# Attention and a rational-activation MLP on one core: bias moved from sigmoids to logarithms, four units masked, new planner costs, contiguous inputs

## The chip, the cores and the metric

The kernel runs on one core of a Trainium2 chip. The metric is the device time of one execution, in microseconds, as the median of a few runs.

## The reference

Two stages follow each other. In the first, 32 learned vectors attend over each batch's 12480 tokens (4 batches, 128 channels), and then the tokens attend over the 32 results. In the second, every token goes through an MLP with 2048 hidden units whose activation is a rational function of h.

```python
def mab(q, kv):
    s = scale * (q @ kv.transpose(0, 2, 1))
    s = s - s.max(-1, keepdims=True)
    a = np.exp(s)
    a /= a.sum(-1, keepdims=True) + 1e-09
    return a @ kv
h = mab(I, x)
return mab(x, h)
...
h = x @ w_in
P = a[0] + a[1] * h + a[2] * h2 + a[3] * h3
Q = 1.0 + np.abs(b[0]) * np.abs(h) + np.abs(b[1]) * h2
g = P / (Q + 1e-6)
return g @ w_out
```

## The kernel before

**The work.** Tokens are cut into tiles of 480 (26 a batch, 104 in all), and the hidden layer into 8 pairs of 128 units. One tile with one pair is a unit, `Unit(b, n, q)`, 832 in all. Since the attention's output is a mix of 32 vectors, `piece` multiplies those vectors with `w_in` once per batch into the stationary matrix `st`, and `first` gets a unit's h by two matmuls of `st` with the 128-row tile `at`, which holds the attention weights of the tile's tokens in parts.

**A unit's way.** `first` (PE) writes h into one of three PSUM banks. Then |h| is taken, in one of two ways. In a unit whose q is not in `MASKED`, the stationary matrix already holds a shift by `k2`, and ACT takes the absolute value with the bias `back` that takes it out again ("abs", `u<-h,all`). DVE then makes the numerator's product D from u and h. In a unit whose q is in `MASKED`, there is no shift; DVE clears the sign bit ("mask", `u<-h` on DVE), or ACT takes a plain absolute value ("taken", `u<-h` on ACT), and POOL prepares u + k1 ("pre", `l<-u,all`) before D (`l<-h,all,l`). For a q that is also in `EXTRA`, PE can instead compute the shifted h a second time from the extra weights `sx` ("again"), and D takes the other form, without "pre". D frees the bank. Next, 1/Q comes as a sigmoid of a logarithm: ACT takes Ln over two units at once ("ln", `u<-u 128x1920`) and then a Sigmoid: two units at once ("sig2"), one ("sig", `u<-u,all 128x960`), or one into a PSUM bank ("sigp", `i<-u,all`). After a sigmoid into PSUM, DVE adds k3 and multiplies ("Ev", `l<-l,all,i`); after the others POOL does, in two instructions ("add", `l<-l,all`, and "Eg", `l<-l,u`). `second` (PE) multiplies the result with `w_out` in two fp32 matmuls of two passes each, adding up over the tile's 8 units in the bank po, and `fetch` copies it out (DVE) and stores it.

Ln and Sigmoid are in different activation tables, so ACT works in batches of up to six pairs: a table load, six Ln, a table load, twelve sigmoids.

**Order.** All engines work in order. The class `Flow` plans the order when the program is built: it keeps a clock per engine, and at each step picks among the events that could come next (`options`), by ready time and by the tables `COST` (how long each event is taken to be), `RANK`, `LOAD`, `GEN` and `WAIT`. `do` emits the instructions. The attention of coming tiles (`tokens`, `quotients`, `spread`) and the next batch's first stage (`induce`) run as generators between the units. Loads go out on SP's queue. `InOrder.do`, line 157, records every instruction of the fast branch, so nearly all rows of the profile name that line.

**The start.** `before()` loads all of batch 0 by columns (`wide_columns`) and by rows (`x_rows`, 512 B runs in `x_t`) and the weights as float64 words, converts these (`words`), computes the first attention, and derives the activation's constants (`Params.derive`): with c2 = ch - 1, the sigmoid has the bias `lnc` = ln(c2) + 2 ln(LAM), one number held in a column of the tile `all`. The logarithm's bias is the constant LAM.

Of the kernel before, what the change touches and what calls it, by code (L numbers as in the profile page):

```python
# [17 lines left out]
P = 128  # L18
# [3 lines left out]
HB = 4  # L22
# [22 lines left out]
class Params:  # L45
# [46 lines left out]
    def derive(self):  # L92

        a0, a1, a2, a3 = self.a
        mult, add, sub, mx = ALU.mult, ALU.add, ALU.subtract, ALU.max
        b0, b1 = self.ts(self.b0, 1e-3, mx), self.ts(self.b1, 1e-3, mx)
        mag3 = self.abs(a3)  # L100
# [12 lines left out]
        r = self.mul(r, self.kappa)
        q1 = self.mul(a1, r)
        r = self.mul(r, self.kappa)
        q0 = self.mul(a0, r)
        self.k1 = self.ts(self.sub(ch, q1), 0.5, mult)
        k12 = self.mul(self.k1, self.k2)
        self.k3 = self.sub(self.ts(self.sub(self.mul(self.k2, ch), q0), 0.5, mult), k12)
        self.back = self.ts(self.k2, -1.0, mult)  # L120
        top = self.mul(self.mul(self.mul(a3, alpha), self.mul(alpha, alpha)), self.recip(gamma))
        self.rho = self.ts(self.mul(top, self.recip(c2)), -2.0, mult)
        self.lin_scale = self.ts(self.mul(c2, self.kappa), -0.5, mult)
        self.lin_shift = self.ts(self.mul(c2, self.k2), -0.5, mult)
        self.lnc = self.new()
        self.nc.scalar.activation(self.lnc, c2, AF.Ln, bias=0.0, scale=1.0)
        self.lnc = self.ts(self.lnc, 2.0 * math.log(LAM), add)
# [52 lines left out]
class Flow:  # L180


    LAT = 0.15
    COST = {"first": 0.52, "second": 1.53, "linear": 0.3, "again": 0.52, "fetch": 0.6, "D": 1.13, "mask": 1.08, "Ev": 1.13, "abs": 0.95, "ln": 1.71, "sig": 1.79, "half": 0.99, "load": 1.4, "pre": 1.1, "add": 1.13, "Eg": 2.22}
    RANK = {"again": 2.9, "first": -30.3, "second": 86.6, "fetch": -52.7, "D": 10.9, "mask": -30, "Ev": -53.2, "abs": 3, "ln": 64.3, "wide": 100, "one": 2, "sig": -64.7, "pre": -41.2, "add": 113.3, "Eg": 74.2, "load": 34, "take": 71.3}
    LOAD = {"v": -2.15, "g": -0.03}
    GEN = {"pe": 3.3, "v": 59.3, "a": 7.9, "g": 26.8, "x": -49.5}
    WAIT = {"pe": 0, "v": 0, "a": 0, "g": 0.2}
    BATCH = 6
# [6 lines left out]
    BANKS = 3  # L196
    FULL = 12.7
    MASKED = (0, 2, 3, 5, 6)
    EXTRA = (2, 5)

# [84 lines left out]
    def options(self):  # L285
# [9 lines left out]
        if self.i1 < len(us) and bank is not None and self.free(self.slots) is not None and (self.i1 % 2 or self.free(self.rooms) is not None):  # L295
            u = us[self.i1]
            at = self.k.ready_at(u)
            if at is not None:
                yield "pe", max(at, bank), R["first"], C["first"], ("first", u)
        if self.i2 < len(us):  # L300
# [16 lines left out]
        for u in self.masks[:1]:  # L317
            yield "a", max(u.t["first"] + LAT, u.room_at), R["take"], C["abs"], ("taken", u)
        for u in self.abss[:1]:
# [28 lines left out]
    def do(self, what, u, start, end):  # L348
# [75 lines left out]
        elif what == "ln":  # L424
            w = us[2 * u]
            A.activation(w.pair, w.pair, AF.Ln, bias=LAM, scale=LAM)
            self.nl += 1
            self.since = end
        elif what == "sig2":
            A.activation(u.pair, u.pair, AF.Sigmoid, bias=p.lnc, scale=-2.0)  # L430
            for w in us[u.n:u.n + 2]:
# [4 lines left out]
        elif what == "sig":  # L436
            A.activation(u.u, u.u, AF.Sigmoid, bias=p.lnc, scale=-2.0)
            u.t["e"] = end + LAT
# [3 lines left out]
        elif what == "sigp":  # L442
            u.bank, _ = self.take(self.banks)
            u.inv = k.hp(u, "i")
            A.activation(u.inv, u.u, AF.Sigmoid, bias=p.lnc, scale=-2.0)
            u.t["e"] = end + LAT
# [40 lines left out]
class Kernel:  # L487

    def __init__(self, ctx, tc, x_t, x_c, ind_c, w_in_d, w_out_d, moe_a, moe_b, out):
        self.tc, self.nc = tc, Engines(tc)  # L490
        self.x_t, self.x_c, self.ind_c, self.w_in_d, self.w_out_d = x_t, x_c, ind_c, w_in_d, w_out_d
        self.moe_a, self.moe_b, self.out = moe_a, moe_b, out
        self.B, _, self.NCH, _ = x_t.shape
        self.NB = self.NCH // HB
        self.NG = -(-self.NB // 4)
        self.F = w_in_d.shape[1]
        self.NF = self.F // P
# [50 lines left out]
    def weights(self):  # L548

        parts = []  # L550
        for f0 in range(0, self.F, BT):
            c = slice(f0, min(f0 + BT, self.F))
            parts.append((self.w_in_d[:, c], self.w_in[:, c], c.stop - c.start))
        for f0 in range(0, self.NF, 3):
            c = slice(f0, min(f0 + 3, self.NF))
            dst = self.w_out[:, c].rearrange("p f d -> p (f d)")
            parts.append((self.w_out_d[:, c].rearrange("p f d -> p (f d)"), dst, C * (c.stop - c.start)))
        for n, (src, dst, width) in enumerate(parts):
            tag, bufs = (self.place("l"), 1) if width > 2 * P else ("oT", 1)
            raw = self.mp.tile([P, width], mybir.dt.int64, tag=tag, name=f"raw{n}", bufs=bufs)  # L560
            self.nc.sync.dma_start(out=raw, in_=src)
            yield raw, dst, width
# [307 lines left out]
    def quotients(self, b, n0, nb, a):  # L870
# [269 lines left out]
```

## Time and profile before

| | before |
|---|---|
| median of 3 runs | 2376.53 us (2374.88 to 2377.35) |
| profiled execution | 2380.21 us, span 2378.4 us |
| PE busy | 2181.4 us, 92% of the span |
| ACT busy | 2149.8 us, 90% |
| DVE busy | 2128.0 us, 89% |
| POOL busy | 2008.2 us, 84% |
| mean granted TensorE clock | 0.958 of full speed |

The span runs from the first to the last instruction; the execution's own time is 1.8 us longer. The profile's views used below are the page with busy time per engine, the groups of instructions by form (busy time, mean length of one), the windows view (busy time of each engine in a stretch), the waits (who waited for whom), the chain of work that ended last, and the DMA view. PE is TensorE's matmuls, DVE VectorE, ACT ScalarE, POOL GpSimd. Matmuls overlap, so PE's busy time is not the time it needs at its peak.

### The profile page before, as it was taken

How to read it: one execution, taken by the hardware profiler on the slowest of the kernel's cores; microseconds unless marked ns; L12 is line 12 of the kernel's file. 1: busy time of each engine (PE TensorE's matmuls, PEld its weight loads, DVE VectorE, ACT ScalarE, POOL GpSimd, SP SyncE). 2: the span in 40 equal slices, each digit the busy share in tenths (PEclk: the TensorE clock that was granted, in tenths of full speed). 3: DMA queues.
4: the chain of work that ended last, by engine and by line, in shares of the span. 5: the costliest groups of instructions: out<-in, count | busy, mean ns of one | idle time of the engine just before them, and what ended most of it. 6: DMA issues, size and time to landing. Idle time of an engine off the chain costs nothing.

```text
span 2378.4 us, 24506 instructions
## 1 busy us (share of the span) xinstructions
PE 2181.4 (92%) x7930; PEld 1209.7 (51%) x7930; DVE 2128.0 (89%) x2289; ACT 2149.8 (90%) x1782; POOL 2008.2 (84%) x1406
## 2 busy tenths in 40 slices
PE   6688999999998999899999999999999998989898
PEld 3454545554554555454555555455455554545444
DVE  5668999999899899998999999999999889979996
ACT  1479999999999999998999999999999989989997
POOL 1268998979999899888999888897999999889995
PEclk7669999999999999999999999999999999999999
DMA  9112212211102222220111122222110111011000
GB/s 282 42 46 75 75 51 75 83 42 40 35 25 77 67 73 75 75 58 25 42 42 59 50 75 75 70 61 61 42 42 21 38 42 42 25 34 34 26 25 19
DMA packets 78640, 133.72 MB, mean 56 GB/s; under 512 B 13544, under 2 KB 63976, under 8 KB 78504
## 3 DMA queue, kind: packets, MB, share of 16 engines
q1 hardware_dynamic: 78504, 132.06, 18.8%
q8 instruction: 66, 1.08, 0.2%
q14 instruction: 70, 0.57, 0.1%
HBM read 80.89 MB, written 25.56 MB: 45 GB/s over the span
## 4 chain that ended last, share of the span: by engine, by line
PE 44%; DVE 23%; ACT 14%; POOL 9%; issue 6%; DMA 1%; SPq 1%; ACTq 0%; DVEq 0%; POOLq 0%
PE po L157 29%; DVE l L157 14%; ACT u L157 9%; PE h L157 9%; POOL l L157 9%; DVE u L157 5%; ACT i L157 3%; PE pd L157 2%; PE ph L157 2%; ACT L157 1%; DVE asm L157 1%; DMA at<-hl 1%; SPq L157 1%; DVE oT L157 1%; PE pl L157 1%
## 5 line engine op out<-in xcount | busy, mean ns | idle before, releaser
L157 PE MATMUL po<-l,w_out 128*128 128x480 f32 x3328 | 1496.8, 583 | 36.8 <-POOL l L157 17.7
L157 POOL TENSOR_TENSOR l<-l,u 128x960 f32<-128x960 f32 x451 | 1011.8, 2244 | 41.9 <-ACT u L157 17.2
L157 PEld LDWEIGHTS po<-l,w_out 128*128 128x128 f32 x3328 | 623.1, 193 | 573.7 <-issue 465.3
L157 PE MATMUL h<-at,st 128*128 128x480 f32 x1664 | 655.7, 488 | 100.0 <-DVE l L157 87.4
L157 ACT ACTIVATE u<-u 128x1920 f32<-128x1920 f32 x416 | 731.0, 1799 | 9.3 <-DVE l L157 8.2
L157 POOL TENSOR_SCALAR l<-u,all 128x960 f32<-128x960 f32 x435 | 464.3, 1069 | 218.2 <-DVE u L157 160.6
L157 DVE TENSOR_SCALAR u<-h 128x960 int32<-128x960 int32 x447 | 508.4, 1150 | 70.4 <-PE h L157 65.6
L157 DVE SCALAR_TENSOR_TENSOR l<-h,all,l 128x960 f32<-128x960 f32 x435 | 520.7, 1208 | 25.9 <-POOL l L157 24.1
L157 DVE SCALAR_TENSOR_TENSOR l<-u,all,h 128x960 f32<-128x960 f32 x397 | 476.0, 1205 | 37.9 <-ACT u L157 28.7
L157 PEld LDWEIGHTS h<-at,st 128*128 128x128 f32 x1664 | 300.5, 194 | 393.2 <-issue 203.7
L157 DVE SCALAR_TENSOR_TENSOR l<-l,all,i 128x960 f32<-128x960 f32 x381 | 450.5, 1207 | 41.9 <-ACT i L157 40.9
L157 POOL TENSOR_SCALAR l<-l,all 128x960 f32<-128x960 f32 x451 | 482.6, 1070 | 1.0
L157 ACT ACTIVATE u<-u,all 128x1920 f32<-128x1920 f32 (+1 forms) x299 | 441.1, 1492 | 0.2
L157 ACT ACTIVATE i<-u,all 128x960 f32<-128x960 f32 x381 | 396.9, 1056 | 31.3 <-DVE l L157 28.3
L157 ACT ACTIVATE u<-h,all 128x960 f32<-128x960 f32 x312 | 327.8, 1051 | 40.0 <-PE h L157 38.8
L157 ACT ACT_TABLE_LOAD x148 | 189.9, 1283 | 3.4 <-PEq L1133 0.7
L157 PEld LDWEIGHTS pd<-HT,xT 128*120 128x120 f32 x832 | 109.1, 196 | 20.7 <-issue 11.7
L157 PE MATMUL pd<-HT,xT 128*120 128x32 f32 x832 | 103.1, 271 | 3.8 <-issue 2.4
L157 ACT ACTIVATE u<-h 128x960 f32<-128x960 f32 x73 | 70.1, 963 | 29.5 <-PE h L157 26.2
L157 DVE COPY oT<-po 128x480 f32<-128x480 f32 x104 | 67.6, 650 | 17.5 <-PE po L157 17.2
L157 PE MATMUL po<-at,st 128*128 128x480 f32 x104 | 80.3, 772 | 0.0
L157 PE MATMUL h<-at,sx 128*128 128x480 f32 x170 | 63.4, 454 | 7.7 <-DVE u L157 6.8
(98 smaller groups left out, 776.6 us busy)
## 6 DMA issues: line engine op xcount, KB each, us to landing
xT<-x_c SPq DMA_DIRECT2D x182, 240.0 KB, 3.3
x<-x_t SPq DMA_DIRECT2D x104, 240.0 KB, 4.3
at<-hl SPq DMA_DIRECT2D x416, 60.0 KB, 2.0
out<-oT SPq DMA_DIRECT2D x104, 240.0 KB, 2.2
xTw<-x_c SPq DMA_DIRECT2D x5, 960.0 KB, 10.5
raw<-w_in SPq DMA_DIRECT2D x4, 480.0 KB, 9.3
raw<-w_out SPq DMA_DIRECT2D x5, 384.0 KB, 9.5
xTw<-x_c SPq DMA_DIRECT2D x2, 480.0 KB, 8.5
```

The lines of the kernel that those rows point to most:

```text
L157: ins = call(*args, **kw)
```

## The change

1. The activation's variable is scaled by `root` = 1/sqrt(c2), found as exp(-0.5 ln c2) with two Newton steps. Then the sigmoid's bias is the number 2 ln(LAM), a constant, and the logarithm's bias becomes `lam` = LAM x root, a column in the tile `all`.
2. `MASKED` goes from (0, 2, 3, 5, 6) to (0, 2, 4, 6), and `EXTRA` is empty: no unit's h is computed twice, and the extra weights are not made.
3. The planner gets other numbers, with `first` and `second` dearer (0.52 to 0.56 and 1.53 to 1.60), a delay of 0.1 ahead of `first`, and a "taken" that is 0.09 cheaper.
4. The attention's addition of 1e-9 to the sums goes from DVE to POOL.
5. `x_t` and both weights are laid out so that each load reads one contiguous block: a partition of an x load reads 2 KB in one run where it read four runs of 512 B.

```diff
+        self.rho = self.ts(top, -2.0, mult)
+        self.lin_scale = self.ts(self.kappa, -0.5, mult)
+        self.lin_shift = self.ts(self.k2, -0.5, mult)
+        root = self.new()
+        self.nc.scalar.activation(root, c2, AF.Ln, bias=0.0, scale=1.0)
+        ln, root = root, self.new()
+        self.nc.scalar.activation(root, ln, AF.Exp, bias=0.0, scale=-0.5)
+        for _ in range(2):
+            step = self.ts(self.mul(self.mul(root, root), c2), -0.5, mult, 1.5, add)
+            root = self.mul(root, step)
...
+        self.kappa = self.mul(self.kappa, root)
+        self.k1, self.k2 = self.mul(self.k1, root), self.mul(self.k2, root)
+        self.k3 = self.mul(self.mul(self.k3, root), root)
+        self.back = self.ts(self.k2, -1.0, mult)
+        self.lam = self.ts(root, LAM, mult)
...
-    COST = {"first": 0.52, "second": 1.53, "linear": 0.3, "again": 0.52, ...
+    COST = {"first": 0.56, "second": 1.60, "linear": 0.35, "again": 0.6, ...
...
-    WAIT = {"pe": 0, "v": 0, "a": 0, "g": 0.2}
+    WAIT = {"pe": 0.1, "v": 0.06, "a": 0, "g": 0.26}
...
-    FULL = 12.7
-    MASKED = (0, 2, 3, 5, 6)
-    EXTRA = (2, 5)
+    FULL = 15.0
+    MASKED = (0, 2, 4, 6)
+    EXTRA = ()
...
-                yield "pe", max(at, bank), R["first"], C["first"], ("first", u)
+                yield "pe", max(at, bank + 0.1), R["first"], C["first"], ("first", u)
...
-            yield "a", max(u.t["first"] + LAT, u.room_at), R["take"], C["abs"], ("taken", u)
+            yield "a", max(u.t["first"] + LAT, u.room_at), R["take"], C["abs"] - 0.09, ("taken", u)
...
-            A.activation(w.pair, w.pair, AF.Ln, bias=LAM, scale=LAM)
+            A.activation(w.pair, w.pair, AF.Ln, bias=p.lam, scale=LAM)
...
-            A.activation(u.pair, u.pair, AF.Sigmoid, bias=p.lnc, scale=-2.0)
+            A.activation(u.pair, u.pair, AF.Sigmoid, bias=2.0 * math.log(LAM), scale=-2.0)
...
-        self.nc.sync.dma_start(out=t, in_=self.x_t[b, :, HB * n:HB * n + HB, :])
+        self.nc.sync.dma_start(out=t, in_=self.x_t[b, n])
...
-        yield "v", 0.4
-        nc.vector.tensor_scalar(out=sm, in0=sm, scalar1=1e-9, scalar2=None, op0=ALU.add)
+        yield "g", 0.25
+        (nc.vector if self.boot else nc.gpsimd).tensor_scalar(out=sm, in0=sm, scalar1=1e-9, scalar2=None, op0=ALU.add)
+        yield "v", 0.2
         nc.vector.reciprocal(out=sm, in_=sm)
...
-        yield from self.piece(0, self.F // 512)
+        if Flow.EXTRA:
+            yield from self.piece(0, self.F // 512)
...
-        "x_t": x.reshape(B, N // TP, TP, C).transpose(0, 2, 1, 3),
+        "x_t": x.reshape(B, N // BT, HB, TP, C).transpose(0, 1, 3, 2, 4),
```

The order moves on every engine. Names below carry batch, tile and pair: `h1_5_2` is h of batch 1, tile 5, pair 2; a last number only tells buffers apart.

PE, batch 1, the first matmuls of tile 10. Before:

```order
L157 MATMUL h1_10_1_5911<-at1_8_2_5768,st_1_3772 128x480 x2
L157 MATMUL h1_10_2_5918<-at1_8_2_5768,st_1_3772 128x480 x2
L157 MATMUL h1_10_3_5927<-at1_8_2_5768,st_1_3772 128x480 x2
L157 MATMUL po1_8_0_5931<-l1_8_0_5583,w_out_93 128x480 x2
L157 MATMUL h1_10_2_5937<-at1_8_2_5768,sx1_4719 128x480 x2
L157 MATMUL po1_8_0_5931<-l1_8_4_5641,w_out_93 128x480 x2
L157 MATMUL h1_10_4_5948<-at1_8_2_5768,st_1_3772 128x480 x2
L157 MATMUL po1_8_0_5931<-l1_8_6_5692,w_out_93 128x480 x2
L157 MATMUL h1_10_5_5961<-at1_8_2_5768,st_1_3772 128x480 x2
```

Now:

```order
L165 MATMUL h1_10_1_5834<-at1_8_2_5710,st_1_3669 128x480 x2
L165 MATMUL h1_10_2_5843<-at1_8_2_5710,st_1_3669 128x480 x2
L165 MATMUL po1_8_0_5848<-l1_8_0_5478,w_out_93 128x480 x2
L165 MATMUL h1_10_3_5854<-at1_8_2_5710,st_1_3669 128x480 x2
L165 MATMUL po1_8_0_5848<-l1_8_2_5503,w_out_93 128x480 x2
L165 MATMUL h1_10_4_5869<-at1_8_2_5710,st_1_3669 128x480 x2
L165 MATMUL po1_8_0_5848<-l1_8_3_5528,w_out_93 128x480 x2
L165 MATMUL h1_10_5_5880<-at1_8_2_5710,st_1_3669 128x480 x2
```

The second computation of h of pair 2 from `sx` is gone, and from pair 2 on a second matmul of tile 8 (`po1_8`) stands between one h and the next.

ACT, batch 1, one group of logarithms between two table loads, with the absolute values of tile 4 and the first of tile 5. Before:

```order
L157 ACT_TABLE_LOAD
L157 ACTIVATE a1_8_4804<-a1_8_4804 120x512
L157 ACTIVATE u1_3_2_4893<-u1_3_2_4893 128x1920
L157 ACTIVATE u1_3_4_4929<-u1_3_4_4929 128x1920
L157 ACTIVATE u1_4_4_5072<-h1_4_4_5074,all_94 128x960
L157 ACTIVATE u1_3_6_4950<-u1_3_6_4950 128x1920
L157 ACTIVATE u1_4_0_5002<-u1_4_0_5002 128x1920
L157 ACTIVATE u1_4_2_5048<-u1_4_2_5048 128x1920
L157 ACTIVATE u1_4_6_5118<-h1_4_7_5125,all_94 128x960
L157 ACTIVATE u1_4_4_5072<-u1_4_4_5072 128x1920
L157 ACT_TABLE_LOAD
L157 ACTIVATE u1_5_0_5148<-h1_5_1_5157,all_94 128x960
```

Now:

```order
L165 ACTIVATE u1_3_6_4901<-u1_3_6_4901,all_94 128x1920
L165 ACTIVATE u1_4_4_5016<-h1_4_5_5034,all_94 128x960
L165 ACTIVATE a1_8_4855<-a1_8_4855 120x512
L165 ACTIVATE u1_4_0_4930<-u1_4_0_4930,all_94 128x1920
L165 ACTIVATE u1_4_2_4977<-u1_4_2_4977,all_94 128x1920
L165 ACTIVATE u1_4_4_5016<-u1_4_4_5016,all_94 128x1920
L165 ACTIVATE u1_4_6_5045<-h1_4_7_5069,all_94 128x960
L165 ACTIVATE e2_1_5089<-pc2_1_5052,nm2_1_5066 128x480
L165 ACT_TABLE_LOAD
L165 ACTIVATE u1_3_2_4836<-u1_3_2_4836 128x1920
L165 ACTIVATE u1_5_0_5079<-h1_5_1_5095,all_94 128x960
L165 ACTIVATE i1_3_4_5114<-u1_3_4_4872 128x2x480
```

The logarithms (`128x1920` in place) carry `all` now and the sigmoids behind the table load don't; the absolute values of odd pairs (`h1_4_5`, `h1_4_7`) stand among the logarithms.

DVE and POOL, batch 1, the quotients of the group of four tiles from tile 8 on. DVE before, and then DVE now:

```order
L157 SCALAR_TENSOR_TENSOR l1_4_7_5124<-u1_4_6_5118,all_94,h1_4_7_5125 128x960
L157 TENSOR_SCALAR asm1_8_5059<-asm1_8_5059 120x16
L157 RECIPROCAL asm1_8_5059<-asm1_8_5059 120x16
L157 TENSOR_SCALAR u1_5_0_5148<-h1_5_0_5150 128x960
L157 SCALAR_TENSOR_TENSOR l1_4_6_5119<-h1_4_6_5120,all_94,l1_4_6_5119 128x960
```

```order
L165 TENSOR_REDUCE asm1_8_5044<-a1_8_4855 120x16
L165 TENSOR_REDUCE mx2_1_5064<-pc2_1_5052 128x1
L165 TENSOR_SCALAR nm2_1_5066<-mx2_1_5064,nm2_0_4646 128x1
L165 SCALAR_TENSOR_TENSOR l1_4_6_5046<-h1_4_6_5047,all_94,l1_4_6_5046 128x960
L165 RECIPROCAL asm1_8_5044<-asm1_8_5044 120x16
L165 TENSOR_SCALAR u1_5_0_5079<-h1_5_0_5081 128x960
```

POOL now:

```order
L165 TENSOR_SCALAR l1_3_1_4831<-l1_3_1_4831,all_94 128x960
L165 TENSOR_SCALAR asm1_8_5044<-asm1_8_5044 120x16
L165 TENSOR_TENSOR l1_3_1_4831<-l1_3_1_4831,u1_3_0_4813 128x960
L165 TENSOR_SCALAR l1_5_0_5080<-u1_5_0_5079,all_94 128x960
L165 TENSOR_TENSOR a1_8_4855<-a1_8_4855,asm1_8_5044 120x512
```

The addition to `asm` left DVE; three DVE instructions now stand between the sum and the reciprocal, and on POOL the addition stands before a multiply of tile 3.

## Rows read from the trace of the kernel before

**Rows 1.** The page, part 1: busy us, share of the span, instructions.

```profile
PE 2181.4 (92%) x7930; PEld 1209.7 (51%) x7930; DVE 2128.0 (89%) x2289; ACT 2149.8 (90%) x1782; POOL 2008.2 (84%) x1406
```

**Rows 2.** Windows: length; busy PE, PEld, DVE, ACT, POOL; PEclk, DMA share, GB/s.

```profile
0.00:200.00 200.00, 142.03 (x694) 88.17 (x694) 127.50 (x285) 97.86 (x98) 82.33 (x69) 0.69 0.41 121
...
200.00:2300.00 2100.00, 1967.87 (x7042) 1085.18 (x7042) 1943.17 (x1953) 1987.42 (x1633) 1877.99 (x1307) 0.98 0.17 51
...
2300.00:2378.40 78.40, 71.50 (x196) 36.33 (x194) 57.33 (x53) 64.55 (x53) 47.84 (x32) 0.98 0.06 20
```

**Rows 3.** Waits, 200 to 2300 us: us in total, times, longest us.

```profile
ACT u L157 <- PE h L157: 47.9, 59, 3.8
...
ACT i L157 <- DVE l L157: 28.0, 46, 3.0
...
DVE l L157 <- ACT u L157: 25.3, 42, 2.2
...
ACT hl L157 <- DMA at<-hl: 18.9, 11, 3.0
```

**Rows 4.** PE: groups by form (busy, mean ns); two chain pieces (start, us).

```profile
L157 PE MATMUL h<-at,sx 128*128 128x480 f32 x170 | 63.4, 454 | 7.7 <-DVE u L157 6.8 <-ACT u L157 0.7
...
2313.23 0.43 PE h L157 x2
...
2313.67 1.61 PE po L157 x4
```

**Rows 5.** Groups by form, ACT: count, busy us, mean ns of one.

```profile
L157 ACT ACTIVATE u<-h,all 128x960 f32<-128x960 f32 x312 | 327.8, 1051 | 40.0 <-PE h L157 38.8 <-POOL l L157 0.2
...
L157 ACT ACTIVATE u<-h 128x960 f32<-128x960 f32 x73 | 70.1, 963 | 29.5 <-PE h L157 26.2 <-POOL l L157 2.8
...
L157 ACT ACTIVATE u<-u 128x1920 f32<-128x1920 f32 x416 | 731.0, 1799 | 9.3 <-DVE l L157 8.2 <-POOL l L157 0.4
...
L157 ACT ACTIVATE u<-u,all 128x1920 f32<-128x1920 f32 x152 | 285.4, 1888 | 0.2
...
L157 ACT ACTIVATE u<-u,all 128x960 f32<-128x960 f32 x147 | 159.3, 1084 | 0.0
...
L157 ACT ACTIVATE i<-u,all 128x960 f32<-128x960 f32 x381 | 396.9, 1056 | 31.3 <-DVE l L157 28.3 <-DVE rs L157 0.7
```

**Rows 6.** Groups by form, DVE.

```profile
L157 DVE TENSOR_SCALAR u<-h 128x960 int32<-128x960 int32 x447 | 508.4, 1150 | 70.4 <-PE h L157 65.6 <-POOL l L157 3.1
...
L157 DVE SCALAR_TENSOR_TENSOR l<-h,all,l 128x960 f32<-128x960 f32 x435 | 520.7, 1208 | 25.9 <-POOL l L157 24.1
...
L157 DVE SCALAR_TENSOR_TENSOR l<-u,all,h 128x960 f32<-128x960 f32 x397 | 476.0, 1205 | 37.9 <-ACT u L157 28.7 <-PE h L157 7.6
...
L157 DVE SCALAR_TENSOR_TENSOR l<-l,all,i 128x960 f32<-128x960 f32 x381 | 450.5, 1207 | 41.9 <-ACT i L157 40.9
...
L157 DVE TENSOR_SCALAR asm<-asm 120x16 f32<-120x16 f32 x23 | 16.0, 696 | 0.1
```

**Rows 7.** Groups by form, POOL.

```profile
L157 POOL TENSOR_TENSOR l<-l,u 128x960 f32<-128x960 f32 x451 | 1011.8, 2244 | 41.9 <-ACT u L157 17.2
...
L157 POOL TENSOR_SCALAR l<-l,all 128x960 f32<-128x960 f32 x451 | 482.6, 1070 | 1.0
...
L157 POOL TENSOR_SCALAR l<-u,all 128x960 f32<-128x960 f32 x435 | 464.3, 1069 | 218.2 <-DVE u L157 160.6 <-ACT u L157 46.7 <-ACT i L157 5.8
...
L157 POOL TENSOR_TENSOR st<-gl,st 64x128 fp32r<-64x128 f32 x4 | 1.8, 457 | 1.0 <-DVE st L157 0.7 <-ACT u L157 0.2
```

**Rows 8.** DMA view, 0 to 70 us: GB/s by slice; issues, us to landing.

```profile
GB/s 0 11 51 271 442 421 421 299 251 263 262 275 351 415 361 235 266 271 400 379 249 258 264 343 381 226 256 270 350 297 243 266 267 277 257 300 146 2 0 0
...
x<-x_t SPq DMA_DIRECT2D x26, 240.0 KB, 10.5
...
xTw<-x_c SPq DMA_DIRECT2D x5, 960.0 KB, 10.5
```

**Rows 9.** Groups by form, DVE, the parameters' products.

```profile
L69 DVE TENSOR_TENSOR all<-all 128x1 f32<-128x1 f32 x35 | 4.4, 151 | 0.3
```

More of the change, by code (lines that the diff above doesn't have):

```diff
@@ L119, in derive @@
         self.k3 = self.sub(self.ts(self.sub(self.mul(self.k2, ch), q0), 0.5, mult), k12)
-        self.back = self.ts(self.k2, -1.0, mult)
         top = self.mul(self.mul(self.mul(a3, alpha), self.mul(alpha, alpha)), self.recip(gamma))
[L122 to L127, printed above, removed]
+        self.rho = self.ts(top, -2.0, mult)
[8 more added lines that the diff above has]
+            root = self.mul(root, step)
         big = self.mul(self.add(self.abs(k12), self.abs(self.k3)), self.recip(ch))
@@ L183 @@
     LAT = 0.15
[L184 to L187, printed above, removed]
-    WAIT = {"pe": 0, "v": 0, "a": 0, "g": 0.2}
+    COST = {"first": 0.56, "second": 1.60, "linear": 0.35, "again": 0.6, "fetch": 0.6, "D": 1.13, "mask": 1.08, "Ev": 1.13, "abs": 0.95, "ln": 1.79, "sig": 1.70, "half": 0.90, "load": 1.4, "pre": 1.06, "add": 1.11, "Eg": 2.22}
+    RANK = {"again": 40, "first": -52.7, "second": 123.6, "fetch": -33.4, "D": 11.7, "mask": -22, "Ev": 1.8, "abs": -15.1, "ln": 19.8, "wide": 56.7, "one": 28.7, "sig": -167.4, "pre": 11.5, "add": 86.9, "Eg": 76.3, "load": 9.6, "take": 38}
+    LOAD = {"v": -0.17, "g": -1.05}
+    GEN = {"pe": 110.4, "v": 80.9, "a": 9.2, "g": 75.8, "x": -14.3}
+    WAIT = {"pe": 0.1, "v": 0.06, "a": 0, "g": 0.26}
     BATCH = 6
@@ L436, in do @@
         elif what == "sig":
-            A.activation(u.u, u.u, AF.Sigmoid, bias=p.lnc, scale=-2.0)
+            A.activation(u.u, u.u, AF.Sigmoid, bias=2.0 * math.log(LAM), scale=-2.0)
             u.t["e"] = end + LAT
@@ L444, in do @@
             u.inv = k.hp(u, "i")
-            A.activation(u.inv, u.u, AF.Sigmoid, bias=p.lnc, scale=-2.0)
+            A.activation(u.inv, u.u, AF.Sigmoid, bias=2.0 * math.log(LAM), scale=-2.0)
             u.t["e"] = end + LAT
@@ L492, in __init__ @@
         self.moe_a, self.moe_b, self.out = moe_a, moe_b, out
-        self.B, _, self.NCH, _ = x_t.shape
+        self.B, self.NCH = x_t.shape[0], x_t.shape[1] * HB
         self.NB = self.NCH // HB
         self.NG = -(-self.NB // 4)
-        self.F = w_in_d.shape[1]
+        self.F = w_in_d.shape[0] // P
         self.NF = self.F // P
@@ L552, in weights @@
             c = slice(f0, min(f0 + BT, self.F))
-            parts.append((self.w_in_d[:, c], self.w_in[:, c], c.stop - c.start))
+            parts.append((self.w_in_d[P * c.start:P * c.stop], self.w_in[:, c], c.stop - c.start))
         for f0 in range(0, self.NF, 3):
@@ L556, in weights @@
             dst = self.w_out[:, c].rearrange("p f d -> p (f d)")
-            parts.append((self.w_out_d[:, c].rearrange("p f d -> p (f d)"), dst, C * (c.stop - c.start)))
+            parts.append((self.w_out_d[P * C * c.start:P * C * c.stop], dst, C * (c.stop - c.start)))
         for n, (src, dst, width) in enumerate(parts):
@@ L560, in weights @@
             raw = self.mp.tile([P, width], mybir.dt.int64, tag=tag, name=f"raw{n}", bufs=bufs)
-            self.nc.sync.dma_start(out=raw, in_=src)
+            self.nc.sync.dma_start(out=raw, in_=src.rearrange("(p n) -> p n", p=P))
             yield raw, dst, width
@@ L934, in ahead @@
             yield from self.linear(b)
-            yield from self.piece(b, self.F // 512)
+            if Flow.EXTRA:
+                yield from self.piece(b, self.F // 512)
     def groups(self, first):
@@ L1122 @@
     B, N, _ = x.shape
+    w, v = moe_w_in.view(np.int64), moe_w_out.view(np.int64).reshape(-1, P, C).transpose(1, 0, 2)
     arrays = {
-        "x_t": x.reshape(B, N // TP, TP, C).transpose(0, 2, 1, 3),
+        "x_t": x.reshape(B, N // BT, HB, TP, C).transpose(0, 1, 3, 2, 4),
         "x_c": x.transpose(0, 2, 1),
         "ind_c": inducing.T,
-        "w_in": moe_w_in.view(np.int64),
-        "w_out": moe_w_out.view(np.int64).reshape(-1, P, C).transpose(1, 0, 2),
+        "w_in": np.concatenate([w[:, f:f + BT].ravel() for f in range(0, w.shape[1], BT)]),
+        "w_out": np.concatenate([v[:, f:f + 3].ravel() for f in range(0, v.shape[1], 3)]),
         "moe_a": moe_a,
```

## The prediction

> **What bounds the kernel now.** I read the page's line of busy times first: four engines stand between 84% and 92%, so none is idle enough to be free [rows 1]. Then the windows view in three stretches, to part the ends from the middle [rows 2]. In the first 200 us ACT is busy for 97.9 us and TensorE's granted clock averages 0.69, between its two levels (1.2 and 2.4 GHz). In the 2100 us between 200 and 2300 the clock is 0.98, and PE is busy for 1967.9 us, ACT for 1987.4, DVE for 1943.2 and POOL for 1878.0. In the last 78.4 us ACT is busy for 64.6. So ACT is the fullest engine of the middle (94.6%), with PE beside it, and ACT's idle time is 102.1 us at the start, 112.6 in the middle and 13.9 at the end, together 228.6, which is the span of 2378.4 less its 2149.8 busy us.
>
> Third the waits of the middle [rows 3]: of ACT's 112.6 us, 47.9 end when PE has written an h, 28.0 when DVE frees a PSUM bank for a sigmoid, and 18.9 when the copies out of hl have landed. The rest is in small waits. PE is pushed late by more than its instructions: a pair of first matmuls takes 0.43 us in the chain's tail and a unit's four passes of second take 1.61 us [rows 4]. The planner wrote down 0.52 and 1.53 for them, so each second, 832 of them, was planned 0.08 us too short, 67 us in all. What a plan leaves out there, the other engines stand and wait for.
>
> **The change, part by part.** Durations are those of one profiled execution (2380.2 us: the span and 1.8 us around it). It stands 3.7 us above the median of the runs, 2376.5, and I take that off at the end.
>
> ACT. Counting instructions in the built order: |h| with a bias goes from 312 to 416, |h| without one from 73 to 16, wide sigmoids from 152 to 158, single ones from 147 to 142, those into PSUM from 381 to 374; the 416 logarithms stay. By [rows 5] that is 104 x 1.051 = +109.3 and 57 x 0.963 = -54.9 us. A bias held in a tensor costs an Abs 1.051 - 0.963 = 0.088 us more than a constant one, both reading PSUM, and the wide sigmoid (tensor) stands 0.089 above the wide logarithm (constant). So the bias that moves into the logarithms costs 416 x 0.088 = +36.6, and the one that leaves 674 sigmoids gives 59.3 back; their changed counts give 1.5 more. Sum for ACT: +30.2 us, of which the bias is -22.7 and the extra |h| +54.4.
>
> PE. The 170 matmuls into h from the extra weights go: 63.4 us of busy time by their row, or 85 pairs x 0.43 = 36.6 us if only their full-speed pace counts [rows 4]. I take the ends as bounds, -37 to -63. In the built order they stood between the h of later pairs, so what goes is also a delay of the h that ACT waits for.
>
> DVE. 47 masks fewer x 1.150 = -54.1; the two forms of D trade 19 at 1.208 and 1.205, nothing; seven fewer products from PSUM x 1.207 = -8.4; the 28 adds of 1e-9 that go to POOL, at 0.696, -19.5 [rows 6]. Sum -82 us.
>
> POOL. Seven units more through add and multiply, 7 x (1.070 + 2.244) = +23.2; 19 pre-adds fewer, 19 x 1.069 = -20.3 [rows 7]. The 28 adds of 1e-9 have no row on POOL: not below zero, since an instruction is added, and not above the 0.457 us of its 64x128 subtraction, 12.8 in all; I take 6, about half, since its 16 elements are an eighth of that tile but an instruction's fixed part remains. Sum about +9 us, under an engine with 222 idle us in the middle.
>
> Start. The loads of x by rows turn from runs of 512 B to runs of 2 KB. In the first 70 us the 26 loads of x take a median of 10.5 us to land for 240 KB each, where the five of 960 KB take the same 10.5. The traffic runs at 421 to 442 GB/s while the large ones go out and at 251 to 263 where eight x loads follow [rows 8]. Those 26 loads are 6.39 MB, 25 us at 257 GB/s and 15 at 430: a gain of 0 to 10 us, if the other engines can follow. They can't wholly, since PE is at a lower clock there, so I take 6. The Trainium skill ("DMA: Bandwidth & Descriptors", section Specifications) speaks against it: it gives 512 B as the smallest transfer at line rate. By that rule this term is nothing and the forecast below would be 6 us higher. The later loads of x lie under the middle's work, where DMA is 17% busy [rows 2], and count for nothing by themselves; but they share the SP queue with the copies out of hl that ACT waits for. The root's Newton steps are nine or ten DVE instructions of 0.15 us more [rows 9] and one activation, placed while the first loads are still under way: nothing, and some 2 us without that cover.
>
> The sum goes by ACT, the fullest engine, as its work plus its idle time. Work 2149.8 + 30.2 = 2180. Idle at the start 102 - 6 = 96, at the end 14. In the middle 112.6 before; PE is relieved by 37 to 63 us, DVE by 82, and PE's true length now stands in the plan. I take two thirds off the wait for h (32), half off that for a bank (14), and half off that for hl's copies (9.5): 57 left. 2180 + 96 + 14 + 57 = 2347 of span, 2349 with what lies around it, **2345** against the median. The idle term is my choice, not a row: its ends are 112.6 (nothing gained) and about 20 (all three waits gone).
>
> **The rivals.** About 0.2%, 5 us, is what a measurement of this kernel can tell from no change.
>
> *ACT pays in full: slower.* Half of all units now take |h| on ACT instead of 385 of 832 passes, and ACT is in order: a pass that finds no h yet holds up the logarithms and sigmoids behind it, and DVE already waits 25.3 us for ACT's u [rows 3]. If the middle's idle stays at 112.6, the sum is 2180 + 96 + 14 + 112.6 + 1.8 - 3.7 = 2401. It decides at 88 us of idle: above that the change is slower than 2376.5. For it speaks that the one engine that was fullest gets more work while the relief goes to others; against it that most of its idle is waiting for just those. Chance 0.16.
>
> *PE was the bound: much faster.* PE is busy for 93.7% of the middle, only just behind ACT, and its 63 us could come off whole: 2376.5 - 63 - 6 = 2308. Against it: at the pace of the tail the 832 pairs and seconds fill 832 x (0.43 + 1.61) = 1697 us [rows 4], so part of its busy time is slack. Chance 0.20 for under 2325.
>
> *DVE waits at the reciprocal.* The add of 1e-9 now sits between two DVE instructions and behind whatever POOL runs; a multiply there is 2.244 us [rows 7]. In the built order three to five other DVE rows stand between, about 3.5 us, so mostly it is covered. If each of the 28 still waited one multiply, +63 us: 2408. Chance 0.03.
>
> *The change doesn't do what it says.* If the 0.089 us belonged to the sigmoid and not to its bias, ACT would keep the 59.3 us and the sum is 2404. The two Abs rows differ in nothing but the bias, so 0.02.
>
> *It cancels.* Idle of 83 to 93 us: within 5 us of 2376.5, chance 0.06.
>
> **How the numbers follow.** Forecast, 2325 to 2371: 0.53. Faster is that and the PE case, 0.73; same 0.06; slower 0.16 + 0.03 + 0.02 = 0.21. The range leaves out the far end of the PE case and the upper half of the slower ones: 2305 to 2390.
>
> **What would show it.** In the changed profile the wide sigmoid should stand near 1.80 us and the wide logarithm near 1.89, single sigmoids near 0.99 and those into PSUM near 0.97; ACT's busy time near 2180, DVE's near 2046, PE's 2118 to 2144. ACT's idle between 200 us and the last 80 should be near 57 and its wait for PE's h near 16. Loads of x should land clearly sooner than 10.5 us in the first 70 us, and the flow's first units should start some 6 us earlier. I am wrong if ACT's busy time rises by less than 15 us, if its share of the middle stays at 94.6%, or if DVE stands idle before the reciprocal of asm for more than a few us in all.

## The result and the profile after

The changed kernel takes **2319.9 us** (2317.4 to 2324.6) where the kernel before, on the same chip, takes 2375.7: a ratio of 0.978 [0.9763, 0.9798], 56 us faster. The forecast was 2345 in a range of 2305 to 2390. The profiled execution stands at 2318.7.

The page's busy times, and the windows view with the same last 80 us apart as before (columns as in [rows 2]):

```profile
PE 2111.2 (91%) x7744; PEld 1160.7 (50%) x7744; DVE 2053.4 (89%) x2204; ACT 2162.6 (93%) x1824; POOL 2009.5 (87%) x1425
```

```profile
0.00:200.00 200.00, 146.83 (x726) 89.48 (x726) 134.63 (x298) 108.01 (x112) 85.60 (x72) 0.76 0.43 125
...
200.00:2236.90 2036.90, 1899.56 (x6851) 1040.12 (x6849) 1866.92 (x1859) 1990.71 (x1660) 1872.19 (x1321) 0.99 0.18 53
...
2236.90:2316.90 80.00, 64.84 (x169) 31.08 (x169) 51.87 (x49) 63.88 (x54) 51.73 (x34) 1.00 0.06 20
```

Against [rows 1] ACT is busy 12.8 us longer, while the span is 61.5 us shorter: ACT's idle time fell from 228.6 to 154.3 us. In the middle it is 2036.9 - 1990.7 = 46.2 us, where it was 112.6 [rows 2]; ACT is busy for 97.7% of it. The waits behind that (200 us to the last 80):

```profile
ACT u L165 <- PE h L165: 13.1, 20, 2.2
...
ACT i L165 <- DVE l L165: 12.8, 24, 1.9
...
ACT hl L165 <- DMA at<-hl: 7.3, 6, 1.8
...
DVE l L165 <- ACT u L165: 51.3, 81, 2.1
...
DVE l L165 <- POOL l L165: 45.1, 63, 1.5
...
PE h L165 <- DVE l L165: 62.5, 103, 3.2
```

ACT's three waits fell from 47.9, 28.0 and 18.9 [rows 3] to 13.1, 12.8 and 7.3. DVE in turn waits twice as long for ACT as before (51.3 against 25.3), so ACT is further ahead as the fullest engine. It is not the only one that sets the pace. The page's chain of work that ended last, before and after, goes over all four engines now, where PE had the largest share and ACT 14%:

```profile
PE 44%; DVE 23%; ACT 14%; POOL 9%; issue 6%; DMA 1%; SPq 1%; ACTq 0%; DVEq 0%; POOLq 0%
```

```profile
ACT 25%; POOL 23%; PE 23%; DVE 16%; issue 8%; DMA 1%; SPq 1%; ACTq 0%; POOLq 0%; DVEq 0%
```

ACT's groups by form, beside [rows 5]:

```profile
L165 ACT ACTIVATE u<-h,all 128x960 f32<-128x960 f32 x416 | 435.8, 1050 | 19.8 <-PE h L165 16.2 <-POOL l L165 2.8 <-PE pa L165 0.3
...
L165 ACT ACTIVATE u<-h 128x960 f32<-128x960 f32 x16 | 15.4, 962 | 3.3 <-PE h L165 3.3
...
L165 ACT ACTIVATE u<-u,all 128x1920 f32<-128x1920 f32 x416 | 774.3, 1892 | 4.8 <-DVE l L165 4.3
...
L165 ACT ACTIVATE u<-u 128x1920 f32<-128x1920 f32 x158 | 281.9, 1796 | 0.2
...
L165 ACT ACTIVATE u<-u 128x960 f32<-128x960 f32 x142 | 140.9, 992 | 0.0
...
L165 ACT ACTIVATE i<-u 128x960 f32<-128x960 f32 x374 | 354.8, 965 | 16.4 <-DVE l L165 14.3 <-PE po L165 0.7 <-PE h L165 0.2
```

The wide logarithm went from 1799 to 1892 ns and the wide sigmoid from 1888 to 1796: the bias held in a tensor costs 92 to 93 ns, whichever of the two functions has it. The Trainium skill ("ScalarE: Activation LUTs", section What ACT_TABLE_LOAD costs) gives 93 ns for a pointer operand, and the trace agrees.

**The start** did not gain. The load of x lands no sooner, and the first h from `at` comes no sooner either (first rows: DMA view, 0 to 70 us, as in [rows 8]; then PE's timeline of the changed kernel, of the kernel before, and of a repeat of the changed kernel that is described with the layout below):

```profile
GB/s 1 10 65 293 445 430 417 247 245 263 259 273 314 413 373 238 251 260 371 402 262 246 251 315 392 245 241 250 294 375 213 248 248 308 207 245 335 56 0 0
...
x<-x_t SPq DMA_DIRECT2D x26, 240.0 KB, 10.6
```

```profile
92.98 2.74 PE L165 MATMUL h<-at,st 128*128 128x480 f32 x6 [3.47 <-DMA at<-hl]
```

```profile
90.72 2.74 PE L157 MATMUL h<-at,st 128*128 128x480 f32 x6 [4.45 <-DMA at<-hl]
```

```profile
89.99 2.74 PE L165 MATMUL h<-at,st 128*128 128x480 f32 x6 [4.11 <-DMA at<-hl]
```

The changed kernel and its repeat lie 3 us apart, on either side of the kernel before, so this difference is one between executions.

The reason why the load did not gain is an error of mine in the description above: the kernel before did not read x in runs of 512 B. Its host array already puts a partition's four rows of a tile side by side, so that a partition's part of a load was 2 KB in one run; only the step from partition to partition changed, from 53,248 B to 2048 B. The page counts the same packets before and after. Between 2 KB and 8 KB it counts 78504 - 63976 = 14528. The 104 loads of x, with 120 partitions each, make 12480 such packets, and the wide loads of batch 0's columns and of the weights make the other 2048; in runs of 512 B the loads of x would not be among them:

```profile
DMA packets 78640, 133.72 MB, mean 56 GB/s; under 512 B 13544, under 2 KB 63976, under 8 KB 78504
```

```profile
DMA packets 78639, 133.70 MB, mean 58 GB/s; under 512 B 13544, under 2 KB 63976, under 8 KB 78504
```

### The profile page after: what moved, and what is told of

Its sections match the earlier page's. It is cut to its first block, busy times and chain, and to the rows that moved or that the text cites. A ratio compares the mean times of both kernels' runs of the same rounds, so it can differ in the third digit from the quotient of the medians.

```text
span 2316.9 us, 24295 instructions
## 1 busy us (share of the span) xinstructions
PE 2111.2 (91%) x7744; PEld 1160.7 (50%) x7744; DVE 2053.4 (89%) x2204; ACT 2162.6 (93%) x1824; POOL 2009.5 (87%) x1425
## 2 busy tenths in 40 slices
DMA packets 78639, 133.70 MB, mean 58 GB/s; under 512 B 13544, under 2 KB 63976, under 8 KB 78504
## 3 DMA queue, kind: packets, MB, share of 16 engines
q1 hardware_dynamic: 78504, 132.06, 19.4%
## 4 chain that ended last, share of the span: by engine, by line
ACT 25%; POOL 23%; PE 23%; DVE 16%; issue 8%; DMA 1%; SPq 1%; ACTq 0%; POOLq 0%; DVEq 0%
POOL l L165 23%; ACT u L165 18%; PE po L165 15%; DVE l L165 10%; ACT i L165 4%; PE h L165 4%; DVE u L165 3%; ACT L165 2%; PE ph L165 2%; SPq L165 1%; PE pd L165 1%; DMA at<-hl 1%; DVE oT L165 1%; DMA xT<-x_c 1%; PE pgt L165 0%
## 5 line engine op out<-in xcount | busy, mean ns | idle before, releaser
L165 PE MATMUL po<-l,w_out 128*128 128x480 f32 x3328 | 1472.1, 576 | 72.2 <-DVE oT L165 40.6
L165 POOL TENSOR_TENSOR l<-l,u 128x960 f32<-128x960 f32 x458 | 1026.7, 2242 | 37.7 <-ACT u L165 12.8
L165 ACT ACTIVATE u<-u,all 128x1920 f32<-128x1920 f32 x416 | 774.3, 1892 | 4.8 <-DVE l L165 4.3
L165 POOL TENSOR_SCALAR l<-u,all 128x960 f32<-128x960 f32 x416 | 444.7, 1070 | 148.8 <-DVE u L165 121.3
L165 DVE SCALAR_TENSOR_TENSOR l<-u,all,h 128x960 f32<-128x960 f32 x416 | 501.0, 1207 | 57.4 <-ACT u L165 56.3
L165 DVE SCALAR_TENSOR_TENSOR l<-h,all,l 128x960 f32<-128x960 f32 x416 | 500.9, 1211 | 50.6 <-POOL l L165 47.8
L165 DVE TENSOR_SCALAR u<-h 128x960 int32<-128x960 int32 x400 | 457.7, 1149 | 44.2 <-PE h L165 37.1
L165 ACT ACTIVATE u<-h,all 128x960 f32<-128x960 f32 x416 | 435.8, 1050 | 19.8 <-PE h L165 16.2
L165 ACT ACTIVATE u<-u 128x960 f32<-128x960 f32 (+1 forms) x300 | 417.9, 1415 | 0.2
L165 ACT ACTIVATE i<-u 128x960 f32<-128x960 f32 x374 | 354.8, 965 | 16.4 <-DVE l L165 14.3
L165 POOL TENSOR_TENSOR cv<-cv 128x384 f32<-128x384 f32 (+2 forms) x11 | 12.2, 1114 | 67.4 <-DVE cv L165 53.4
L165 ACT ACTIVATE e<-pc,nm 128x480 f32<-128x480 f32 (+1 forms) x28 | 18.4, 657 | 50.3 <-DVE nm L165 47.2
```

The costliest lines, as they stand in the source:

```text
L165: ins = call(*args, **kw)
```

## The experiments

Three theories were tried. T1: the time is ACT's work and its idle time, and the idle time shrinks as PE and DVE are relieved. T2: the relief of PE and DVE counts by itself. T3: the plan's order did it. Each median stands beside the ratio to the kernel before on the same chip, with its 95% interval. The kernel before itself had medians from 2370.3 to 2375.7 in the four series, so a few microseconds between medians of different series need not mean anything.

### The bias alone, in either order

In the kernel before, only `derive`, the logarithm and the sigmoids as changed:

```diff
-            A.activation(w.pair, w.pair, AF.Ln, bias=LAM, scale=LAM)
+            A.activation(w.pair, w.pair, AF.Ln, bias=p.lam, scale=LAM)
...
-            A.activation(u.pair, u.pair, AF.Sigmoid, bias=p.lnc, scale=-2.0)
+            A.activation(u.pair, u.pair, AF.Sigmoid, bias=2.0 * math.log(LAM), scale=-2.0)
...
```

> The kernel before with the scaled parameters alone: constant bias in the 680 sigmoids, tensor bias in the 416 logarithms; its order is word for word the one before. Theory 'ACT's work and idle time' (T1): ACT has 680 x 0.088 - 416 x 0.088 = 23 us less work and is the fullest engine, so about -15 to -23 us, 2353 to 2361. Rival 'the relief of PE and DVE did it' (T2): ACT is not what the others wait for, within 5 us of 2376. Rival 'the plan did it' (T3): within 5 us of 2376 too, since the order is the old one.

And in the changed kernel, the same undone:

> The changed kernel with the old parameters: tensor bias in the sigmoids (674), constant in the logarithms (416); the order is the changed kernel's. T1: ACT is fuller than before (93% of the span, 97.7% of the middle), so its 23 us come back nearly whole: 2338 to 2344. T2 and T3: within 5 us of 2320.

Measured: 2369.5, ratio 0.9987 [0.9971, 1.0003], in the old order; 2340.3, ratio 0.9864 [0.9827, 0.9900], in the new one, 20 us above the changed kernel. The pages of the first and the second:

```profile
PE 2170.7 (92%) x7930; PEld 1204.4 (51%) x7930; DVE 2127.9 (90%) x2298; ACT 2130.6 (90%) x1783; POOL 2009.4 (85%) x1406
```

```profile
PE 2122.1 (91%) x7744; PEld 1161.4 (50%) x7744; DVE 2051.5 (88%) x2195; ACT 2185.4 (94%) x1823; POOL 2009.5 (86%) x1425
```

ACT's busy time moves by 19.2 us in the first case (from 2149.8) and by 22.8 in the second (from 2162.6). In the old order next to nothing comes of it: T1's 15 to 23 us fail there, T2 and T3 hold, and ACT's idle time is 2366.8 - 2130.6 = 236.2 us, more than before. In the new order nearly all of it counts, as T1 said and T2 and T3 did not.

### Masks and planner numbers, one without the other

Kernel before with the new masks (without the extra pieces) and the old numbers; kernel before with the new numbers and the old masks:

```diff
-    MASKED = (0, 2, 3, 5, 6)
-    EXTRA = (2, 5)
+    MASKED = (0, 2, 4, 6)
+    EXTRA = ()
```

> The kernel before with the masked units (0, 2, 4, 6) and nothing computed twice, the old planner numbers used for the new order. |h| on ACT goes from 385 to 452 passes (+73 us), masks on DVE from 447 to 380 (-77 us), 170 matmuls of PE go (-37 to -63 us). T1: ACT's 73 us are more than the idle time that PE and DVE can give back (about 55): 2380 to 2400. T2: 2313 to 2340. T3: within 10 us of 2376.

> The kernel before with the new planner numbers alone (costs, ranks, loads, waits, FULL, the 0.1 ahead of first); the same masks and second computations as before, of which 146 matmuls remain. ACT's work stays within 10 us. T1: waits for h shrink since PE's length is in the plan, but PE keeps its work: -10 to -25 us, 2350 to 2366. T2: within 5 us of 2376. T3: -40 to -56 us, 2320 to 2336.

The changed kernel with the old numbers, and with the old masks:

> The changed kernel with the planner numbers of before (its order is made anew from them). |h| on ACT 453 passes instead of 432, masks on DVE 379 instead of 400. T1 (ACT's work and idle time): ACT has 22 us more work, and waits for h come back as PE is planned too short: 2345 to 2365. T2 (the relief of PE and DVE did it): 2320 within 8. T3 (the plan did it): 2350 to 2376.

> The changed kernel with the masked units (0, 2, 3, 5, 6) and the second computation for 2 and 5, under the new planner numbers. |h| on ACT falls from 432 to 391 passes (-41 us), masks on DVE rise from 400 to 441 (+47 us), PE gets 162 matmuls back (+35 to 60 us). T1: what ACT saves is about what its waits take back: 2310 to 2335. T2: PE and DVE decide: 2355 to 2376. T3: 2320 within 8.

| bias of the changed kernel | old numbers | new numbers |
|---|---|---|
| old masks | 2369.5 (addition of 1e-9 on DVE) | 2403.9, 1.013 [1.0095, 1.0166] |
| new masks | 2408.2, 1.0143 [1.0104, 1.0182] | 2319.9, 0.978 [0.9763, 0.9798] |

In the kernel before itself the new masks alone give 2392.7, 1.0085 [1.006, 1.011], and the new numbers alone 2417.0, 1.0177 [1.015, 1.0203]. Either half alone makes the kernel slower, and only both together make it faster. The new masks alone fall where T1 put them (2380 to 2400) and refute T2 (2313 to 2340): PE and DVE were relieved and it is slower. T3, within 10 us of 2376, misses it too. The page of that run shows why:

```profile
PE 2145.4 (90%) x7744; PEld 1175.1 (49%) x7744; DVE 2059.8 (86%) x2219; ACT 2213.0 (93%) x1855; POOL 1953.9 (82%) x1365
```

ACT has 63.2 us more work than before, for the added passes, and in a span of 2388.6 us it is idle for 175.6, which is 53.0 less. So the relief of PE and DVE did reach ACT's waits, by about the 55 us that T1 had put down, and the added passes took back more.

The other three fall above T1's ranges: the new numbers alone by 51 us, the changed kernel with the old numbers by 43, and with the old masks by 69. T2 and T3 miss them too. The page of the changed kernel with the old numbers, and two of its waits (200 us to the last 80), show where the relief went:

```profile
PE 2148.4 (89%) x7744; PEld 1177.5 (49%) x7744; DVE 2060.3 (86%) x2202; ACT 2190.4 (91%) x1855; POOL 1950.3 (81%) x1387
```

```profile
ACT u L165 <- PE h L165: 55.4, 60, 5.5
...
DVE u L165 <- PE h L165: 65.7, 79, 12.2
```

PE has only 37 us more busy time than in the changed kernel, yet ACT waits 55.4 us for h where it waits 13.1 there, and DVE's masks wait 65.7, up to 12.2 at once. The old numbers also give ACT 37 plain |h| passes, not 16. With the old masks in the changed kernel, the new numbers also rank the second computation of h, which the change never makes, so that cell says less of the plan as such. Nor does one run say much of a set of numbers: with new masks and old numbers, ACT was idle for 175.6 us in the kernel before, and for 2405.6 - 2190.4 = 215.2 in the changed kernel. Between these two only the bias, the place of the addition and the inputs differ, and the order that was made anew for them.

### What in the numbers counts

The changed kernel with PE as cheap in the plan as before, with PE dearer still, and with the old ranks:

```diff
-    COST = {"first": 0.56, "second": 1.60, ...
+    COST = {"first": 0.52, "second": 1.53, ...
...
-                yield "pe", max(at, bank + 0.1), R["first"], C["first"], ("first", u)
+                yield "pe", max(at, bank), R["first"], C["first"], ("first", u)
```

> The changed kernel with PE as cheap in the plan as before: first 0.52 and second 1.53, no 0.1 ahead of first; the rest of the planner's numbers are the new ones. |h| on ACT 444 passes against 432. Theory C (true costs): the plan is short of PE's length again by 0.04 + 0.07 us a unit, 92 us in all, and ACT's wait for h rises from 13 us towards the 48 of before: 2340 to 2365. Theory P (a tuned point): any step off the numbers costs, here as much as with PE dearer still. Theory N (PE's costs do little): 2320 within 8.

```diff
-    COST = {"first": 0.56, "second": 1.60, ...
+    COST = {"first": 0.60, "second": 1.67, ...
```

> The changed kernel with PE dearer still in the plan: first 0.60 and second 1.67 (the chain shows 0.43 and 1.61). |h| on ACT 442 passes against 432. Theory C (true costs): what was right becomes a little too long, waits for h stay near 13 us: 2315 to 2335, and clearly below the run with PE cheap. Theory P (a tuned point): as far above 2320 as the run with PE cheap, 2335 or more. Theory N: 2320 within 8.

> The changed kernel with RANK, LOAD and GEN of before, and the new costs, waits and FULL. |h| on ACT 453 passes against 432 (+22 us). Theory C (true costs): most of the gain stays, ACT's extra passes are what is lost: 2335 to 2350. Theory P (the ranks belong to these masks and costs): as bad as with all the old numbers, 2390 to 2410.

Measured: 2367.8, 0.9983 [0.9969, 0.9998]; 2381.1, 1.0023 [1.0005, 1.0041]; 2369.3, 0.9984 [0.9964, 1.0005]. Each of the three steps off the new numbers costs 48 to 61 us, whichever way PE's cost is moved. The true-cost theory fails with PE dearer: it asked for 2315 to 2335, clearly below PE cheap, and it is above. The theory of a tuned point holds for both PE runs; of the ranks it asked for 2390 to 2410, which they miss on the good side. The planner's other new numbers (the costs of ACT's and POOL's events, `WAIT`, `FULL`) were not tried by themselves. The pages of the three, and ACT's wait for h (200 us to the last 80), for PE cheap, then PE dear, then the old ranks:

```profile
PE 2128.2 (90%) x7744; PEld 1170.4 (49%) x7744; DVE 2030.2 (86%) x2183; ACT 2177.4 (92%) x1833; POOL 2041.9 (86%) x1443
...
ACT u L165 <- PE h L165: 30.3, 43, 7.6
```

```profile
PE 2150.6 (90%) x7744; PEld 1172.7 (49%) x7744; DVE 2051.6 (86%) x2205; ACT 2175.1 (91%) x1836; POOL 1975.0 (83%) x1403
...
ACT u L165 <- PE h L165: 39.3, 32, 8.3
```

```profile
PE 2134.9 (90%) x7744; PEld 1166.8 (49%) x7744; DVE 2034.7 (86%) x2184; ACT 2183.6 (93%) x1847; POOL 2008.5 (85%) x1423
...
ACT u L165 <- PE h L165: 29.1, 32, 4.3
```

Waiting is only a part of what these steps cost. Their plans also give ACT more |h| passes, and its busy time is 14.8, 12.5 and 21.0 us above the changed kernel's; its idle time (span less busy time) is 32.8, 50.0 and 21.8 us above.

### The addition of 1e-9

The changed kernel with that instruction on DVE at the place the plan had for it:

```diff
-        (nc.vector if self.boot else nc.gpsimd).tensor_scalar(out=sm, in0=sm, scalar1=1e-9, scalar2=None, op0=ALU.add)
+        nc.vector.tensor_scalar(out=sm, in0=sm, scalar1=1e-9, scalar2=None, op0=ALU.add)
```

> The changed kernel with the attention's 28 additions of 1e-9 back on DVE, each right where the plan put it for POOL; all other engines' orders stay word for word, save that POOL's list lacks them. DVE +28 x 0.70 = 20 us, POOL -28 x 0.25 = 7 us. T1 (ACT is the bound): little of it is seen, 2318 to 2328. T2 (DVE's work counts in full): 2335 to 2340.

Measured: 2336.8, 0.9847 [0.9818, 0.9876], 17 us above the changed kernel. T1 in this narrow form fails: DVE's work counts although ACT is the fullest engine. T2's number came, but its sum did not: the additions took longer than the 0.70 us put down for them, DVE's busy time rose by 28.9 us (2053.4 to 2082.3), and 17 of these were seen. The page, and the instruction on DVE here and on POOL in the changed kernel (the tile's view: min/median/max ns):

```profile
PE 2120.8 (91%) x7744; PEld 1163.0 (50%) x7744; DVE 2082.3 (89%) x2232; ACT 2165.5 (93%) x1824; POOL 2002.6 (86%) x1397
```

```profile
L165 DVE TENSOR_SCALAR asm<-asm x29: 160/1305/2212, 83.8 to 2186.6; 120x16 f32<-120x16 f32 x23, 120x8 f32<-120x8 f32 x4, 120x4 f32<-120x4 f32 x1, 120x12 f32<-120x12 f32 x1
```

```profile
L165 POOL TENSOR_SCALAR asm<-asm x28: 237/252/253, 113.1 to 2165.1; 120x16 f32<-120x16 f32 x23, 120x8 f32<-120x8 f32 x4, 120x12 f32<-120x12 f32 x1
```

And what PE and ACT wait for in it (200 us to the last 80):

```profile
PE h L165 <- DVE l L165: 69.2, 107, 3.3
...
ACT i L165 <- DVE l L165: 19.7, 34, 1.9
ACT u L165 <- PE h L165: 19.4, 27, 2.3
```

ACT's work is the same within 3 us; its waits for h and for banks rose by 6.3 and 6.9 us over the changed kernel's. PE's own wait for DVE ahead of an h rose from 62.5 to 69.2. So DVE's extra time reaches ACT through the instructions that free the banks.

### The layout

Old layout of x in the changed kernel, and (by intent) a flat access to it, which turned out to be the changed kernel's own access (78640 packets on the page against 78639), so that it is a repeat of it:

```diff
-        self.nc.sync.dma_start(out=t, in_=self.x_t[b, n])
+        self.nc.sync.dma_start(out=t, in_=self.x_t[b, :, HB * n:HB * n + HB, :])
...
-        "x_t": x.reshape(B, N // BT, HB, TP, C).transpose(0, 1, 3, 2, 4),
+        "x_t": x.reshape(B, N // TP, TP, C).transpose(0, 2, 1, 3),
```

> The changed kernel with the old layout of x alone; same order. As the profile has it (same packets, same landing times) it is the same within 3 us of 2320. If the new layout did gain something at the start or on SP's queue, 2325 or more.

> The changed kernel with each load of x written as two-dimensional, so that a partition's 2 KB are one run for the DMA too; its order is word for word that of the changed kernel. In the changed kernel's profile the packets and the landing time of x did not move (10.6 us against 10.5 in the first 70 us). If the runs stayed 512 B there: packets under 2 KB drop by some 37000, x lands in 6 to 8 us in the first 70 us, SP issues one in about 0.4 instead of 1.3 us, and the start is 3 to 8 us shorter: 2312 to 2317. If 2 KB are no faster than four runs of 512 B: 2320 within 3.

Measured: 2319.7, 0.977 [0.9737, 0.9803], and 2319.4, 0.9775 [0.9752, 0.9799]. The layout of x is worth nothing that these runs can tell: the old one and the repeat lie within 1 us of the changed kernel's median, with intervals of some 8 us either way. The weights' layout was not tried alone.

## Why the prediction was right, and where it was not

**The range held; the stretch thought likeliest did not.** The direction was right, and the forecast was 25 us too high. 2319.9 lies under the 2325 to 2371 that had the chance 0.53, where 0.20 was given to PE as the bound. That mechanism did not come: with the 170 matmuls gone and the old numbers the kernel got slower (2392.7).

**The terms.** ACT's work plus its idle time is the span whatever happens, so only the terms could fail: 2180 + 96 + 14 + 57. Measured: 2162.6 of work, 92 idle us in the first 200, 16 in the last 80, 46 between. The largest term that I chose, a middle idle of 57, came out at 46, and each of the three waits near its forecast (16, 14 and 9.5 against 13.1, 12.8 and 7.3). The 30 us by which the span was missed are 17 of work, 11 of the middle and 4 of the start, less 2 at the end; against the medians 25 are left, since this profiled execution lies 1.2 us below its median where the one before lay 3.7 above. The rival "ACT pays in full" (idle staying at 112.6) did not come. Of my three signs of being wrong one came: ACT's busy time rose by 12.8 us, less than 15.

**ACT's work was mis-sized by 17 us.** The groups' busy times add to +32.6 us (forecast 30.2): +108.0 and -54.7 for |h|, +43.3 for logarithms, -3.5, -18.4 and -42.1 for sigmoids. But ACT's busy time as a whole rose by 12.8 only, since an instruction that waits for nothing starts before the one ahead has ended. All of ACT's groups add to 92.3 us more than its busy time before, and to 112.4 more now. That the 20 us come of fewer waits and 42 more instructions fits, but is argued. ACT's timeline of the changed kernel (start, length):

```profile
998.55 1.90 ACT L165 ACTIVATE u<-u,all 128x1920 f32<-128x1920 f32 x1
...
1000.34 1.06 ACT L165 ACTIVATE u<-h,all 128x960 f32<-128x960 f32 x1
...
1001.28 0.64 ACT L165 ACTIVATE a<-a 120x512 f32<-120x512 f32 x1
```

The first ends at 1000.45 and the second starts at 1000.34; the second ends at 1001.40, the third starts at 1001.28. So instruction lengths, added up, overstate the work.

**The start failed.** The term "a gain of 0 to 10 us", taken as 6, rested on runs of 512 B that were not there. By the rule of the Trainium skill that I had set against it the term is nothing, and it measured nothing; but with 2 KB runs on both sides no run here tests that rule. That ACT's idle time in the first 200 us fell from 102 to 92 all the same, near the 96 of the sum, is luck. ACT is busy for 1.9 us less than before in the first 100 us, and for 12.1 more in the second, behind the first h; and with the old layout of x the idle time is 94.8.

**The reason for the idle time was half wrong.** That PE and DVE are relieved did count: the new masks alone cut ACT's idle time by 53 us. It is not enough, since their added passes cost more. "PE's true length now stands in the plan" has no base in its own rows: a second was planned 0.08 us short there, but a pair of first 0.09 us long (0.52 against 0.43), so the two together were planned at 2.05 us where the trace has 2.04 [rows 4]; and the new numbers put first further off, at 0.56. Nor do the two PE runs bear it out as it was told: with PE cheap ACT's wait for h comes back to 30 us, but with PE dearer still, where nothing of PE is left out, to 39. For second alone, where 1.60 is next to the trace's 1.61, they can't tell a true cost from a tuned one. What the runs show is that masks and numbers fit each other: of nine orders, the one before, this one and seven others, this one has the least idle time of ACT in it (154.3 us; the next has 175.6). Why these numbers and not their neighbours do so stays open; I did not take the order apart further.

**What no run parts from the order: TensorE's clock.** The granted clock, a mean between the two levels of 1.2 and 2.4 GHz, rose from 0.958 of full speed to 0.975, in the first 200 us from 0.69 to 0.76 and in the middle from 0.98 to 0.99. PE's busy time fell by 70.2 us, more than my bound of 63. In 25 executions of the kernel before on one chip the mean went from 0.956 (2384.2 us) to 0.969 (2367.7 and 2371.2), the longer ones mostly at the lower clock; a straight line through them gives 1.2 us for 0.001. The changed kernel's four, at 0.972 to 0.975, lie too close together to test it. By that line the changed kernel's clock, 0.974 in the mean of four against 0.961, would stand for about 15 of the 56 us, an estimate. The waits of PE that the order leaves may set the clock, so whether this is a part of the order's gain or one beside it stays open.

**DVE and POOL.** DVE's busy time fell by 74.6 us (forecast 82) and POOL's rose by 1.3 (forecast 9). The rival of a wait at the reciprocal did not come: POOL's addition takes 0.252 us and DVE idles 0.2 us ahead of the reciprocal in all. That small step is worth 17 us in this order, which I had as 19.5 us of DVE's work and not as a gain of its own. Back on DVE, the additions raised DVE's busy time by 28.9 us there.

## What to carry to other kernels

Where several engines run in an order planned ahead, the worth of a part depends on the waiting in that order: some 20 us of ACT's work were worth 1 to 3 us (7 at most by the interval) in the order with 112 us of middle idle, and 20 us in the one with 46. Judge such a part in the order that it will run in, with the plan made anew for it, and do not take one half of a joint change for its whole. And read a transfer's real access before pricing a layout: the packet counts on the page, set against the number of loads and partitions, tell it.

## What the runs showed of the hardware

The addition of 1e-9, on 16 elements a partition mostly, took a median of 1305 ns and up to 2212 on DVE, in the run that put it back there, against 252 ns on POOL. On DVE it lasted as long as POOL's instruction beside it. Of the 29 additions, 20 started while a POOL instruction ran, and each of these ended 0.02 to 0.04 us after that one; the other nine took 0.16 to 0.17 us. One of the first kind, with POOL's multiply, and one of the second, between two POOL instructions (timelines of that run: start, length):

```profile
754.06 2.21 DVE L165 TENSOR_SCALAR asm<-asm 120x16 f32<-120x16 f32 x1
...
754.02 2.22 POOL L165 TENSOR_TENSOR l<-l,u 128x960 f32<-128x960 f32 x1
```

```profile
1012.53 0.16 DVE L165 TENSOR_SCALAR asm<-asm 120x16 f32<-120x16 f32 x1
...
1011.00 1.07 POOL L165 TENSOR_SCALAR l<-u,all 128x960 f32<-128x960 f32 x1 [0.43 <-DVE u L165]
1013.85 1.07 POOL L165 TENSOR_SCALAR l<-u,all 128x960 f32<-128x960 f32 x1 [1.78 <-DVE u L165]
```

The Trainium skill ("SBUF — State Buffer", section Who interferes with whom) tells of a pair of ports that DVE and GpSimd share, which, with DVE in a mode that uses both, the one that issues first holds for its whole instruction. The trace agrees, by the times at which these additions end; the mode itself is not in it.
